# Pooled attention with a gated MLP on one core: the four hand-written issue lists are put in another order

## The chip, the core and the metric

The kernel runs on one core of a Trainium2 chip. The time is that of one execution on the device, in microseconds (us). The engines are PE (TensorE, matrix products; PEld is its weight load), DVE (VectorE), ACT (ScalarE), POOL (GpSimd) and SP (SyncE, which here issues nearly all DMAs). Each engine takes its own instructions strictly in the order in which the program lists them, and waits on semaphores for the results of the others.

## The reference

Eight batches of attention over pooled keys, then one gated MLP that mixes along the sequence. In the sizes of this case B = 8, H = 8, S = 576, D = 64, so x has 512 features:

```python
k_p = k.reshape(B, H, S // 8, 8, D).mean(axis=3)      # 72 keys a head
v_p = v.reshape(B, H, S // 8, 8, D).mean(axis=3)
scores = (q @ k_p.transpose(0, 1, 3, 2)) / sqrt(D)
attn = exp(scores - max(scores)); attn /= attn.sum(-1) + 1e-9
x = (attn @ v_p).transpose(0, 2, 1, 3).reshape(B, S, 512)
h = gelu_tanh(x @ w_in)                               # 512 x 1024
u, v = h[..., :512], h[..., 512:]
v_n = (v - mean(v)) / sqrt(var(v) + 1e-6) * g_ln
v_s = einsum('ts,bsd->btd', w_sg, v_n) + b_sg         # 576 x 576
out = x + (u * v_s) @ w_out                           # 512 x 512
```

Results are float32. The products that need it are made of high and low halves: an operand is split by ACT (the rounded high half) and by DVE or POOL (what is left), and three products are added in PSUM.

## The kernel before, in words

The work of one batch is cut into steps, and each step is a Python generator (`step_A` at line 359 to `step_Z` at line 900) that issues one stage up to each `yield`. The steps, with a number for the tile or head pair:

- A, B and C load a pair of k, of v, or a group of q; E loads the rows `left` over by the pooling (all DMAs go through `load`, line 211, on SP). lv, lu, lo, ls and lb load weights.
- K and P pool k and v: in batch 0 by PE, later by a DVE reduction (line 387). Q transposes q (on DVE at line 492, in batch 0 by PE at 484 with an ACT copy at 487).
- S makes the scores of two heads: five products into a PSUM tile, the negated maximum `nmax` on DVE (510), ten exponentials on ACT (529), then on DVE the sum, the reciprocal and the product `e` (538 to 547), after which the PSUM tile is given back; POOL copies the leftover columns `el` (555). Batches 0 and 1 use a variant with one large exponential.
- T transposes e on PE (161) and splits it with ACT `ah` (591) and DVE `al` (598); L does the same for the leftover columns. V multiplies with v; ACT copies the result out (626, 628), POOL takes the low half (630), ACT copies the end of the sequence to `xtails` (632).
- H is the product for one of five row tiles of the v half, 12 matmuls of 512 columns, followed by Gelu on ACT (669), the norm on DVE and POOL (674 to 680), and the split `vk` (ACT 683, POOL 685). U is the product of a quarter of the u half, 24 matmuls of 288 columns, followed by Gelu (700). Exp and Gelu need different activation tables, so a change from one to the other on ACT brings a table load.
- W is the product along the sequence, 28 matmuls of 288 columns, and the gating on DVE (744, 746; for the last batch 725 and 726, then a split by ACT 731 and POOL 734). G builds sums of the gated tiles for batches 1 to 6 on POOL and ACT (760 to 776), which let O make the output with seven products of half tiles instead of eight. O adds its products to x on DVE (832; batch 0 at 891, batch 7 at 868).
- Z transposes 128 columns of the output on DVE (910) and then issues four stores of 72 KB on SP. The buffer of the transpose is a quarter of `umem`, one for even and one for odd Z: Z3 can be transposed when the stores of Z1 have landed, Z2 when those of Z0 have.

The order is written out by hand in four lists at the top: PROLOGUE (batch 0 and the start of 1 and 2), FIRST (the rest of batch 1's period), PERIOD (issued for b = 2 to 6) and LAST (b = 7). A token names the step and, behind the sign, the batch relative to the list's own: `S3+1` is the next stage of step S3 of the next batch. Lower-case tokens prepare weights (`lv0` loads, `v0` is a stage of the split). A token whose batch lies outside 0 to 7, or whose step is finished, issues nothing. `emit` (939) walks a list and `advance` (919) or `weight` (925) issues the next stage, so that one list fixes the order on all engines at once. Dependencies that only order the issue then pin each engine to that order.

```python
free = [0, 1, 2, 3]
def take():
    n = free.pop(0)
    return n, psum.tile([P, 2, NB], F32, name="ps", tag=f"ps{n}")
def give(n):
    free.append(n)
```

There are four PSUM tiles of two banks. `take` (117) hands out the tile that was given back longest ago in the order of the list, and `give` (122) returns one. So the list also decides which step inherits whose tile: the first matmul of the new owner waits until the last reader of the former owner is done with it.

Of the kernel before, what the change touches and what calls it, by code (L numbers as in the profile page):

```python
# [20 lines left out]


PROLOGUE = """
lv0 E0+0 v0 A0+0 K2+0 A1+0 K0+0 C0+0 v0 v0 K1+0 v1 K0+0 v0 Q0+0 v1 C1+0 E1+0 v1 C3+0 K1+0 K2+0 P2+0 Q1+0 Q0+0 K2+0
S0+0 v0 S0+0 v1 Q1+0 S1+0 S0+0 Q3+0 S0+0 S1+0 C2+0 S1+0 S0+0 S0+0 Q2+0 Q3+0 ls0 S1+0 S0+0 S3+0 S0+0 S1+0 Q2+0 S2+0
S0+0 B1+0 S3+0 S3+0 S2+0 s4 v1 lv1 S3+0 S1+0 S1+0 s2 S1+0 T0+0 S2+0 s3 T0+0 s2 S2+0 S3+0 s3 S3+0 S3+0 S3+0 P1+0 s3 s2
s4 B0+0 A0+1 v3 S3+0 E0+1 S2+0 v3 s1 S1+0 v2 S2+0 S2+0 A1+1 S2+0 s1 s4 T3+0 C0+1 s1 P0+0 K0+1 S2+0 P2+0 T1+0 B0+1 K2+1
L0+0 T1+0 T2+0 v2 L0+0 V0+0 v3 V1+0 T2+0 K1+1 C1+1 V0+0 s0 V2+0 T3+0 v2 V1+0 s0 K2+1 v2 V0+0 v3 K2+1 V2+0 v2 Q0+1 lu0
V3+0 V0+0 V1+0 P0+1 s0 V1+0 S0+1 Q1+1 S0+1 S0+1 S1+1 C2+1 V3+0 S0+1 v3 S1+1 C3+1 V2+0 V3+0 u0 H0+0 u1 S1+1 u0 u1 S0+1
S1+1 H0+0 lu1 u1 u1 V2+0 S0+1 Q2+1 u0 S1+1 u0 S1+1 H2+0 V3+0 H2+0 u1 u0 H4+0 Q3+1 H1+0 S1+1 u3 H2+0 S0+1 H4+0 S3+1  # L30
T0+1 H4+0 S0+1 u2 u3 C0+2 H1+0 u2 lb0 H2+0 U1+0 H4+0 H3+0 u2 C1+2 T0+1 H4+0 u3 H1+0 u2 T0+1 u3 u3 B1+1 U1+0 P1+1 S3+1
P2+1 H3+0 S2+1 u2 H0+0 lo0 A0+2 S3+1 U3+0 S2+1 S3+1 S2+1 H3+0 S3+1 S2+1 S2+1 H0+0 U3+0 S3+1 H0+0 H4+0 U0+0 H3+0 S2+1
S1+1 H1+0 lo1 U2+0 S3+1 H2+0 H3+0 H4+0 H0+0 S2+1 H1+0 U0+0 U2+0 S3+1 S2+1 L0+1 L0+1 Q0+2 C2+2 K0+2 H1+0 L0+1 o1 T1+1
L0+1 H4+0 H2+0 H3+0 P2+1 o0 o1 o0 W3+0 P2+1 P2+1 W2+0 W3+0 o0 V0+1 W2+0 A1+2 o0 T1+1 o1 o1 o0 T1+1 o2 o1 W0+0 K1+2
V0+1 o2 T2+1 o2 o3 E0+2 V1+1 o2 W0+0 V1+1 o3 o3 W1+0 T2+1 K2+2 T2+1 V1+1 T3+1 Q1+2 K2+2 B0+2 W2+0 W0+0 K2+2 W3+0 W1+0
V2+1 T3+1 S0+2 W1+0 W2+0 S1+2 V2+1 W0+0 P0+2 W1+0 V1+1 Q2+2 S0+2 o3 O1+0 T3+1 S1+2 W3+0 O1+0 O1+0 B1+2 O0+0 S0+2 O0+0
o2 P1+2 S1+2 Z1+0 O0+0 O2+0 C0+3 V3+1 S0+2 S1+2 Z0+0 C3+2 V3+1 S2+2 A0+3 A1+3 O2+0 V0+1 P2+2 S0+2 V2+1 V3+1 H2+1 S2+2
o3 Q3+2 S2+2 V3+1 O2+0 Z0+0 H2+1 T0+2
""".split()
FIRST = """  # L40
A0+2 r0 K0+2 r0 P2+1 U2+0 r0 K1+2 H2+0 H1+0 S2+1 r0 B1+2 H3+0 H1+0 V0+0 S1-4 V2+0 Z2-1 P2+1 Z1-1 r0 H4+0 H1+0 H3+0
T0+1 H4+0 O3-1 r1 r1 r1 H3+0 Z1-11 U2+0 H1+0 H1+0 S2-3 O3-1 H2+0 A1-2 H4+0 H4+0 r1 O3-1 H1+0 H0+0 H4+0 Z3-1 Z2-1 S2+1
H3+0 H0+0 H0+0 Z3-1 U1+0 H4+0 S1+1 H3+0 S3+1 r3 S2+0 S3+1 H4+0 O0-3 P2+1 U1+0 H4+0 H3+0 U3+0 S3+1 W0-7 E0+2 H0+0 H0+0
S3+1 r3 Q3-5 H2+0 H0+0 H2+0 r3 U0+0 S0-2 Q0+2 r3 U3+0 W1+0 U0+0 T0-22 S3+1 W1+0 L0+1 C0-2 L0+1 r2 W0+0 W3+0 S1-5 r2 r2
K2+2 r2 r2 W0+0 L0+1 T0+1 W3-3 G1+0 V0+1 C1+2 W2+0 Q2-2 G0+0 P1+2 V0+1 T1+1 W3+0 L0+1 W2+0 G0+0 S0-1 G1+0 K2+2 O0+0
G1+0 T1+1 T1+1 K2+2 V0+1 W0-2 V1+1 P0-1 P2-7 T2+1 G2+0 O1+0 G4+0 V1+1 S0+2 W0-10 T2+1 O0+0 W1-5 G2+0 G2+0 G2+0 T2+1
V2+1 G2+0 V2+1 G3+0 Q1+2 G4+0 O1+0 O0+0 S2-3 G3+0 O1+0 S0+2 S0+2 G3+0 O0+0 O2+0 G4+0 C3+2 O1+0 T3+1 T3+1 V2+1 G4+0
O2+0 Z1+0 V3-1 G4+0 C2+2 T3+1 O0+0 W1-7 W2-7 O0+0 S1+2 V1+1 V3+1 Z0+0 Z1+0 S1+2 V3+1 O0+0 Z0+0 O0+0 V1-18 Z3+0 B0+2
Z2+0 W1+0 V3+1 Z3+0 Z2+0
""".split()  # L50
# [19 lines left out]


# [910 lines left out]
```

## Time and profile before

| | us |
|---|---|
| median of 3 runs (range) | 571.95 (571.55 to 572.54) |
| profiled execution, its own time | 572.45 |
| span of that execution | 570.4 |
| busy: PE, DVE, ACT, POOL | 544.5, 407.3, 371.5, 306.4 |

The span runs from the first to the last instruction of the profiled execution; some 2 us lie around it. A stretch that the text calls a period is one pass of PERIOD, measured from one batch's matmuls of 120 in a row to the next's. The granted clock of PE is 1.00 in every stretch with matmuls. In a timeline or a chain the columns are the start in us, the duration in us and the instruction, with a count where equal ones follow each other; square brackets give the idle time of the engine just before and what ended it.

### The profile page before, as it was taken

Reading aid. Unit: us, or ns where it says so; the run is one execution under the profiler, and the core shown is the slowest. Engines: PE = TensorE matmul, PEld = TensorE weight load, DVE = VectorE, ACT = ScalarE, POOL = GpSimd, SP = SyncE. Lnnn points to the kernel's source line nnn. Section 1 sums busy time; section 2 is a strip of 40 time slices with the busy share of each in tenths; the row PEclk is TensorE's granted clock in tenths of the full one; section 3 lists DMA queues with packets and bytes.
Section 4 is the critical chain, followed back from the end, with each engine's and each line's share of the span. In section 5 each row is a group of like instructions: output and inputs, shape, how many; then the busy total and the mean of one; then the engine's idle time right before and its main releaser. Section 6 shows DMA issues by size and latency. Waiting matters only on the chain.

```text
span 570.4 us, 10342 instructions
## 1 busy us (share of the span) xinstructions
PE 544.5 (95%) x3721; PEld 510.0 (89%) x3721; DVE 407.3 (71%) x591; ACT 371.5 (65%) x979; POOL 306.4 (54%) x366
## 2 busy tenths in 40 slices
...
GB/s 235 321 147 179 250 70 83 116 65 67 30 1 86 191 12 69 2 105 161 1 68 26 140 102 31 38 64 193 11 68 1 122 20 1 1 34 51 1 1 83
DMA packets 161602, 46.33 MB, mean 81 GB/s; under 512 B 149072, under 2 KB 149072, under 8 KB 161552
## 3 DMA queue, kind: packets, MB, share of 16 engines
...
q8 instruction: 29, 0.48, 0.4%
...
## 4 chain that ended last, share of the span: by engine, by line
PE 52%; DVE 18%; ACT 11%; DMA 6%; issue 5%; SPq 4%; POOL 3%; POOLq 0%; DVEq 0%; ACTq 0%
PE ps L126 49%; SPq L211 4%; DMA kvraw<-in_v 4%; ACT e L529 4%; DVE vp L387 2%; PE ps L161 2%; DVE nmax L510 2%; DVE e L547 2%; DVE ps L744 1%; ACT gk L760 1%; DVE qT L492 1%; DVE kp L387 1%; POOL umem L776 1%; ACT L529 1%; DVE al L598 1%
## 5 line engine op out<-in xcount | busy, mean ns | idle before, releaser
L126 PE MATMUL ps<-wsh,vk 128*128 128x288 f32 x512 | 97.1, 297 | 0.0
L126 PE MATMUL ps<-xhlk,wih 128*128 128x288 f32 x512 | 90.3, 299 | 3.0 <-DVE e L547 2.9
L126 PE MATMUL ps<-wih,xhlk 128*128 128x512 f32 x256 | 85.1, 399 | 1.3 <-DVE e L547 1.3
L126 PEld LDWEIGHTS ps<-xhlk,wih 128*128 128x128 f32 x512 | 75.3, 189 | 4.6 <-ACT vk L683 3.5
L529 ACT ACTIVATE e<-ps,nmax 128x72 f32<-128x72 f32 x240 | 72.9, 338 | 8.5 <-DVE nmax L510 8.3
L126 PEld LDWEIGHTS ps<-wsh,vk 128*128 128x128 f32 x512 | 78.2, 189 | 0.2 <-PE ps L126 0.2
L126 PEld LDWEIGHTS ps<-wih,xhlk 128*128 128x128 f32 x256 | 48.1, 188 | 13.5 <-DVE e L547 2.4
L126 PE MATMUL ps<-wsl,vk 128*128 128x288 f32 x256 | 57.4, 296 | 0.0
L126 PE MATMUL ps<-xhlk,wil 128*128 128x288 f32 x256 | 55.1, 297 | 0.0
L685 POOL TENSOR_TENSOR vk<-xmem,vk 128x512 fp32r<-128x512 f32 x32 | 41.3, 1297 | 25.6 <-ACT vk L683 25.6
L762 POOL TENSOR_TENSOR gk<-umem,gk 128x576 fp32r<-128x576 f32 x18 | 25.7, 1429 | 53.7 <-ACT gk L760 53.7
L529 ACT ACTIVATION_READ_ACCUMULATOR e<-ps,nmax 128x1 f32 x240 | 53.9, 225 | 0.0
L677 POOL TENSOR_TENSOR rstd<-mv,eps 128x1 f32<-128x1 f32 (+1 forms) x40 | 9.6, 241 | 79.2 <-DVE mv L675 75.9
L630 POOL TENSOR_TENSOR xhlk<-xmem,xhlk 128x576 fp32r<-128x576 f32 x32 | 45.4, 1427 | 11.4 <-ACT xhlk L628 11.4
L126 PE MATMUL ps<-wil,xhlk 128*128 128x512 f32 x128 | 50.7, 396 | 0.0
L126 PE MATMUL ps<-gk,woh 128*128 128x288 f32 x224 | 46.8, 300 | 0.6 <-POOL gk L734 0.3
L832 DVE TENSOR_TENSOR xmem<-ps,xmem 128x576 f32<-128x576 f32 x42 | 31.3, 756 | 20.6 <-PE ps L126 20.3
L126 PE MATMUL ps<-kbd,qT 128*128 128x144 f32 x320 | 43.9, 288 | 2.2 <-ACT qT L487 1.3
L126 PEld LDWEIGHTS ps<-kbd,qT 128*128 128x128 f32 x320 | 41.4, 190 | 3.9 <-ACT qT L487 1.7
L126 PEld LDWEIGHTS ps<-wsl,vk 128*128 128x128 f32 x256 | 42.2, 189 | 0.0
L126 PEld LDWEIGHTS ps<-xhlk,wil 128*128 128x128 f32 x256 | 41.1, 189 | 0.0
L762 POOL TENSOR_TENSOR vk<-umem,vk 128x576 fp32r<-128x576 f32 x24 | 34.0, 1426 | 8.0 <-ACT vk L760 7.0
...
## 6 DMA issues: line engine op xcount, KB each, us to landing
...
```

The costliest lines, as they stand in the source:

```text
L126: nc.tensor.matmul(o, lhsT, rhs, start=start, stop=stop, **flags)
L161: nc.tensor.transpose(ps[:rows, i * P:(i + 1) * P], src(i), ident if i < NT - 1 else swap)
L211: queue.dma_start(o, i)
L387: nc.vector.tensor_reduce(out=o, in_=t.rearrange("p a (r d) -> p a d r", r=POOL), axis=AX.X, op=ALU.add)
L510: nc.vector.tensor_reduce(out=nmax, in_=every.rearrange("p s (h k) -> p s h k", h=2), axis=AX.X, op=ALU.max, negate=True)
L529: nc.scalar.activation(e[:, i, h], slots[i][:, h], AF.Exp, bias=nmax[:, i, h:h + 1], **acc)
L547: (nc.gpsimd if (b, g) in MUL_POOL else nc.vector).tensor_tensor(e, e, rec.unsqueeze(3).broadcast_to([P, NT, 2, SP]), op=ALU.mult)
L630: nc.gpsimd.tensor_tensor(xhl[:, 1, g], x32[:, g], xhl[:, 0, g].bitcast(F32), op=ALU.subtract)
L677: nc.gpsimd.tensor_tensor(rstd, mv[:, 1:2], eps[:n, 1:2], op=ALU.add)
L685: (nc.gpsimd if i < NT - 1 else nc.vector).tensor_tensor(lo, vg, hi.bitcast(F32), op=ALU.subtract)
L762: nc.gpsimd.tensor_tensor(lo, x, hi.bitcast(F32), op=ALU.subtract)
L832: nc.vector.tensor_tensor(x, ps[:, :, 0:HALF], x, op=ALU.add)
```

## The change

The four lists are replaced by lists with another order of the same stages. No step, instruction, buffer or shape is changed; the tokens that issue nothing differ. PERIOD and LAST stand here in full, of PROLOGUE and FIRST the beginning.

```diff
--- before
+++ after
 PROLOGUE = """
-lv0 E0+0 v0 A0+0 K2+0 A1+0 K0+0 C0+0 v0 v0 K1+0 v1 K0+0 v0 Q0+0 v1 C1+0 E1+0 v1 C3+0 K1+0 K2+0 P2+0 Q1+0 Q0+0 K2+0
-S0+0 v0 S0+0 v1 Q1+0 S1+0 S0+0 Q3+0 S0+0 S1+0 C2+0 S1+0 S0+0 S0+0 Q2+0 Q3+0 ls0 S1+0 S0+0 S3+0 S0+0 S1+0 Q2+0 S2+0
-S0+0 B1+0 S3+0 S3+0 S2+0 s4 v1 lv1 S3+0 S1+0 S1+0 s2 S1+0 T0+0 S2+0 s3 T0+0 s2 S2+0 S3+0 s3 S3+0 S3+0 S3+0 P1+0 s3 s2
...
+lv0 v0 A1+0 E0+0 v1 A0+0 K1+0 C0+0 v0 K1+0 E1+0 v0 K0+0 K0+0 K2+0 K2+0 Q0+0 P2+0 K2+0 Q0+0 C1+0 v1 Q1+0 v0 S0+0 S0+0
+C2+0 v1 lv1 Q2+0 C3+0 Q1+0 v1 S1+0 S0+0 S1+0 v1 S0+0 Q2+0 S1+0 Q3+0 S0+0 S2+0 v0 S0+0 S0+0 S0+0 S1+0 S1+0 ls0 S2+0
+Q3+0 B1+0 S3+0 S1+0 v3 B0+0 T0+0 S2+0 S1+0 T0+0 s2 S0+0 s2 v3 v3 S1+0 E0+1 s1 S3+0 A0+1 S3+0 S2+0 s4 S3+0 s1 s4 P1+0
...
 """.split()
 FIRST = """
-A0+2 r0 K0+2 r0 P2+1 U2+0 r0 K1+2 H2+0 H1+0 S2+1 r0 B1+2 H3+0 H1+0 V0+0 S1-4 V2+0 Z2-1 P2+1 Z1-1 r0 H4+0 H1+0 H3+0
...
+H1+0 V0+0 Z2-1 H1+0 S1-1 S1+1 r0 Q3-6 P2-5 H3+0 C0-4 S3+1 r0 r0 H3+0 S2-1 K0+2 H1+0 V1-24 r0 V2+0 H2+0 O3-1 W0-13 S1-3
...
 """.split()
 PERIOD = """
-B1+1 Q2+1 H2+0 V2+0 S1+1 H2+0 S0+1 H1+0 S2+1 U3+0 H1+0 P0+1 S2+1 S0+1 Q3+1 C0+2 V3+0 S1+1 H1+0 V1+0 P1+1 H0+0 S2+1
-H2+0 T0+1 W1-13 U3+0 S1+1 H0+0 V0+0 T0+1 H1+0 S2+1 H2+0 S3+1 S3+1 H1+0 H4+0 S3+1 H0+0 H3+0 T0+1 H4+0 S3+1 U1+0 H4+0
-H1+0 H2+0 H2+0 S2+1 A0+2 H3+0 U0+0 P2+1 H3+0 H4+0 U2+0 U1+0 H4+0 P2+1 H0+0 K0+2 W0-9 H3+0 P2+1 H4+0 H0+0 U2+0 C1+2
-S3+1 L0+1 H3+0 H4+0 U0+0 L0+1 H0+0 H4+0 L0+1 P2+1 H3+0 W1+0 W1+0 W0+0 V0+1 Q0+2 W0+0 A1+2 W3+0 E0+2 K2+2 G0+0 K1+2
-W3+0 Q1+2 W2+0 G0+0 T1+1 G1+0 G1+0 V0+1 K2+2 T1+1 L0+1 W2+0 G2+0 G1+0 T1+1 K2+2 O0+0 V0+1 G2+0 T2+1 V1+1 G4+0 G2+0
-T2+1 O1+0 G4+0 T2+1 W2-10 V1+1 G2+0 G2+0 V2+1 T3+1 V2+1 O1+0 G3+0 O0+0 O1+0 O0+0 T3+1 T3+1 O0+0 O1+0 C2+2 O2+0 O0-4
-S0+2 O2+0 G3+0 Z1+0 S0+2 G4+0 G3+0 S1+2 B0+2 O0+0 Z0+0 O0+0 G4+0 Z1+0 V3+1 S0+2 V3+1 G4+0 Z0+0 W3-12 C3+2 V1+1 O0+0
-S1+2 O0+0 Z3+0 Z3+0 V2+1 V3+1 Z2+0 Z2+0
+S1+1 S0+1 S1+1 H2+0 H1+0 S1+1 Q2+1 S0+1 H2+0 H0+0 S1+1 S1+1 V2+0 V1+0 S2+1 V0+0 B0+1 V3+0 H0+0 H1+0 P1+1 S2+1 H1+0
+S2+1 P0+1 H3+0 H4+0 H1+0 H3+0 C0+2 U0+0 H2+0 H0+0 S2+1 C3+1 H2+0 U3+0 H4+0 T0+1 P2+1 U0+0 H4+0 A1+2 H4+0 P2+1 H2+0
+H4+0 P2+1 T0+1 S0+1 Q3+1 H3+0 U3+0 H0+0 H0+0 T0+1 H0+0 U1+0 H4+0 P2+1 H4+0 S3+1 H3+0 H1+0 H4+0 H1+0 U2+0 H3+0 C1+2
+K1+2 E0+2 U2+0 S3+1 S3+1 A0+2 U1+0 H2+0 H3+0 W1+0 S2+1 K0+2 S3+1 K2+2 S3+1 O0-1 W0-1 W0+0 L0+1 W0+0 W1+0 L0+1 G0+0
+L0+1 W2+0 K2+2 G1+0 W2+0 G0+0 K2+2 W3+0 G1+0 L0+1 T1+1 W3+0 G2+0 G1+0 V0+1 O1+0 T1+1 G2+0 W2-1 V0+1 G2+0 G4+0 G4+0
+T1+1 O1+0 G2+0 Q0+2 O0+0 T2+1 V1+1 O1+0 T2+1 T2+1 B1+2 T3+1 G2+0 V1+1 W1-9 O0+0 G3+0 G4+0 V2+1 T3+1 G3+0 W3-8 O0+0
+G4+0 T3+1 C2+2 O2+0 O0+0 G3+0 O0+0 O1+0 O2+0 V3+1 Z0+0 G4+0 S0+2 V1+1 O0+0 V2+1 Z0+0 V0+1 O0+0 Z1+0 V3+1 Q1+2 S0+2
+O0+0 Z1+0 Z3+0 Z2+0 V2+1 Z2+0 Z3+0 V3+1
 """.split()
 LAST = """
-S3+9 V1+0 T2+26 V3+0 H2+0 V0+0 H0+0 H0+0 V2+0 H1+0 V1-1 H1+0 C2-2 S3-1 L0+8 S3+1 B0+4 Q3-10 H4+0 H1+0 H1+0 H4+0 H1+0
-H0+0 P1+1 L0-1 H2+0 H1+0 H3+0 T1+12 S2-12 T2+7 S1+2 V2+5 S0+5 H2+0 T2+12 S2-11 Q2-8 H4+0 H0+0 U3+0 U3+0 H3+0 Q1+1 S0+6
-B1+12 U1+0 H3+0 H4+0 T1-20 V0-17 H0+0 V1+11 H4+0 S1+1 S0+1 U2+0 V1-4 V3+15 V3+10 V3-21 V2-3 T3-10 V0+3 H2+0 S2-15
-Q0+12 S1+5 C3+1 P2-10 K2+4 H3+0 H3+0 P2-2 H3+0 H4+0 U0+0 S3+11 H0+0 U2+0 T3-2 H4+0 K1+10 H2+0 L0+21 T3+14 H4+0 H2+0
-P2+1 A1-11 U0+0 L0+12 K2+24 U1+0 W0+0 W1+0 T0-12 W0+0 W2+0 S2-2 W2+0 W2+0 S0-12 W0+0 C1+4 W2+0 W0+0 W3+0 O1+0 S3-7
-W3+0 W1+0 O0+0 T0-14 S1+9 O1+0 W3+0 V2-10 W3+0 Z1+0 O0+0 W1+0 K0-5 V0+6 Z0+0 W1+0 K2+0 O0+0 Z0+0 A0+3 E0-13 C0+1 O3+0
-S0-11 O3+0 O1+0 S2+2 Z3+0 O2+0 P2-10 T0-12 T1+9 O3+0 S1+8 Z1+0 P0-1 Z3+0 O2+0 O2+0 Z2+0 Z2+0
+U2+0 H0+0 P1+9 V2+0 T2+6 V0-1 C0+8 Q2+4 P0+8 K2-1 H3+0 H3+0 L0+18 H3+0 H1+0 T3+7 V0+0 U2+0 H2+0 V3+0 L0+16 T1-24 K2+30
+V1+0 H1+0 S1+4 H1+0 S0+3 T1+7 H0+0 H0+0 H2+0 T0-20 H1+0 V3+9 H4+0 V0-17 T2+27 H2+0 H2+0 S2-18 H1+0 T0-20 B0+4 V1+15
+U1+0 S3+12 P2+4 H2+0 L0-4 H0+0 H3+0 H0+0 A1-8 H4+0 S1+2 T1+13 E0-15 H2+0 U1+0 H0+0 H3+0 K1+6 H4+0 U0+0 S3-10 K2+7 T3-5
+H3+0 V0+3 Q0-2 U3+0 H4+0 V1-5 C3-2 V3-13 H4+0 P2-23 H4+0 S0-23 U0+0 H4+0 H4+0 H1+0 S3-1 L0+13 W0+0 V3+17 T2+13 S3-19
+A0-2 S3+5 S0-7 S1+17 W1+0 W1+0 W0+0 U3+0 B1+25 W2+0 W0+0 W3+0 V2-9 S2-4 W0+0 W2+0 V2+5 S1+7 S2+0 S2-17 W2+0 V1-9 S1-1
+S2-6 W3+0 K0+9 Q3-5 W2+0 P2-5 W1+0 Q1+1 W3+0 O0+0 T0-14 O0+0 C1-1 O1+0 O1+0 Z1+0 T3+1 Z0+0 W1+0 W3+0 O3+0 V2+0 O0+0
+O1+0 Z1+0 C2-4 O3+0 S0+8 Z0+0 O3+0 O2+0 O2+0 Z3+0 Z3+0 O2+0 S0+16 Z2+0 P2-5 Z2+0
 """.split()
```

Three places that are hard to find in the lists: in PROLOGUE `A1+0` comes before `E0+0`, and `lv1` before `C3+0` and `ls0`; in PERIOD the end now runs `Z1+0` (transpose), `Q1+2`, `S0+2`, `O0+0`, `Z1+0` (stores), `Z3+0`, `Z2+0`; in LAST the four stages of `W0` (product, gate, and the split by ACT and by POOL) now come before the gate of `W2`, and the products are listed `O0 O0 O1 O1` where it was `O1 O0 O1 O0`.

## Rows read from the trace of the kernel before

**Rows 1.** Part 1 of the page: busy time of each engine and instructions.

```profile
PE 544.5 (95%) x3721; PEld 510.0 (89%) x3721; DVE 407.3 (71%) x591; ACT 371.5 (65%) x979; POOL 306.4 (54%) x366
```

**Rows 2.** Stretches: length, then busy PE, PEld, DVE, ACT, POOL, PEclk, DMA share, GB/s.

```profile
0.00:109.00 109.00, 93.50 (x634) 84.90 (x635) 93.91 (x125) 77.69 (x147) 72.14 (x100) 1.00 0.65 173
...
109.00:212.99 103.99, 102.67 (x695) 96.30 (x694) 75.13 (x113) 75.40 (x233) 64.79 (x77) 1.00 0.38 73
...
212.99:279.15 66.16, 65.04 (x451) 61.35 (x449) 48.64 (x70) 47.37 (x138) 32.49 (x38) 1.00 0.36 73
279.15:344.69 65.54, 65.31 (x451) 61.51 (x449) 49.18 (x71) 47.40 (x138) 32.85 (x39) 1.00 0.36 73
344.69:411.75 67.06, 65.72 (x451) 61.41 (x449) 49.18 (x71) 47.50 (x138) 32.84 (x39) 1.00 0.36 72
411.75:478.08 66.33, 65.32 (x451) 61.52 (x449) 48.29 (x72) 47.49 (x138) 33.15 (x39) 1.00 0.25 46
250.00:260.00 10.00, 10.00 (x60) 8.92 (x59) 8.25 (x14) 9.48 (x41) 1.28 (x5) 1.00 0.82 143
...
478.08:566.00 87.92, 86.96 (x606) 82.99 (x603) 42.13 (x74) 28.66 (x53) 38.10 (x39) 1.00 0.16 24
```

**Rows 3.** Waits of PE, whole span: us in total, times, longest.

```profile
PE ps L126 <- DMA kvraw<-in_k: 8.4, 1, 8.4
PE ps L126 <- DVE e L547: 4.2, 5, 1.1
PE ps L126 <- ACT qT L487: 1.3, 2, 1.0
```

**Rows 4.** Chain of waits at 345 us, and the commonest matmul on the page.

```profile
344.94 16.09 PE ps L126 x120
...
L126 PE MATMUL ps<-wsh,vk 128*128 128x288 f32 x512 | 97.1, 297 | 0.0
```

**Rows 5.** SP's timeline to 4.2 us, and the chain of waits there: start, us.

```profile
1.24 1.60 SPq L211 DMA_DIRECT2D left<-in_k  x2
2.89 1.91 SPq L211 DMA_DIRECT2D kvraw<-in_k  x3
...
3.55 4.74 DMA kvraw<-in_k
...
8.43 5.26 PE ps L126 x32
```

**Rows 6.** Chain of waits from 396 to 405.6 us.

```profile
397.95 0.82 DVE nmax L510
...
398.85 1.28 ACT L529
...
400.14 3.14 ACT e L529 x20
...
403.77 0.92 DVE e L547
```

**Rows 7.** PE's timeline at 404 us; in brackets its idle time and the releaser.

```profile
404.82 0.76 PE L126 MATMUL ps<-xhlk,wih 128*128 128x288 f32 x4 [1.00 <-DVE e L547]
```

**Rows 8.** Stores and transposes: timelines of SP and DVE, chain of waits.

```profile
243.57 4.25 SPq L211 DMA_DIRECT2D out<-umem  x8
...
249.51 1.44 DVE L910 STREAM_TRANSPOSE umem<-xmem 128x576 f32<-128x576 f32 x2
...
379.37 3.87 DMA out<-umem
...
383.42 0.78 DVE L910 STREAM_TRANSPOSE umem<-xmem 128x576 f32<-128x576 f32 x1 [1.06 <-DMA out<-umem]
```

**Rows 9.** PE's timeline at 506 and at 552 us.

```profile
506.72 1.46 PE L126 MATMUL ps<-vk,wbk 128*128 128x288 f32 x9 [0.37 <-POOL vk L762]
...
552.36 0.53 PE L126 MATMUL ps<-gk,woh 128*128 128x288 f32 x2 [0.32 <-POOL gk L734]
```

**Rows 10.** Part 2 of the page: GB/s moved, in 40 slices of the span.

```profile
GB/s 235 321 147 179 250 70 83 116 65 67 30 1 86 191 12 69 2 105 161 1 68 26 140 102 31 38 64 193 11 68 1 122 20 1 1 34 51 1 1 83
```

More of the change, by code (lines that the diff above doesn't have):

```diff
@@ L23 @@
 PROLOGUE = """
-lv0 E0+0 v0 A0+0 K2+0 A1+0 K0+0 C0+0 v0 v0 K1+0 v1 K0+0 v0 Q0+0 v1 C1+0 E1+0 v1 C3+0 K1+0 K2+0 P2+0 Q1+0 Q0+0 K2+0
-S0+0 v0 S0+0 v1 Q1+0 S1+0 S0+0 Q3+0 S0+0 S1+0 C2+0 S1+0 S0+0 S0+0 Q2+0 Q3+0 ls0 S1+0 S0+0 S3+0 S0+0 S1+0 Q2+0 S2+0
-S0+0 B1+0 S3+0 S3+0 S2+0 s4 v1 lv1 S3+0 S1+0 S1+0 s2 S1+0 T0+0 S2+0 s3 T0+0 s2 S2+0 S3+0 s3 S3+0 S3+0 S3+0 P1+0 s3 s2
-s4 B0+0 A0+1 v3 S3+0 E0+1 S2+0 v3 s1 S1+0 v2 S2+0 S2+0 A1+1 S2+0 s1 s4 T3+0 C0+1 s1 P0+0 K0+1 S2+0 P2+0 T1+0 B0+1 K2+1
-L0+0 T1+0 T2+0 v2 L0+0 V0+0 v3 V1+0 T2+0 K1+1 C1+1 V0+0 s0 V2+0 T3+0 v2 V1+0 s0 K2+1 v2 V0+0 v3 K2+1 V2+0 v2 Q0+1 lu0
@@ L29 @@
[L29 to L38, printed above, removed]
+lv0 v0 A1+0 E0+0 v1 A0+0 K1+0 C0+0 v0 K1+0 E1+0 v0 K0+0 K0+0 K2+0 K2+0 Q0+0 P2+0 K2+0 Q0+0 C1+0 v1 Q1+0 v0 S0+0 S0+0
@@ new lines @@
+C2+0 v1 lv1 Q2+0 C3+0 Q1+0 v1 S1+0 S0+0 S1+0 v1 S0+0 Q2+0 S1+0 Q3+0 S0+0 S2+0 v0 S0+0 S0+0 S0+0 S1+0 S1+0 ls0 S2+0
+Q3+0 B1+0 S3+0 S1+0 v3 B0+0 T0+0 S2+0 S1+0 T0+0 s2 S0+0 s2 v3 v3 S1+0 E0+1 s1 S3+0 A0+1 S3+0 S2+0 s4 S3+0 s1 s4 P1+0
+v2 P0+0 s2 P2+0 S2+0 S2+0 S3+0 S2+0 s3 S3+0 s0 S3+0 S2+0 s3 v3 S3+0 S1+0 s4 S2+0 s1 C1+1 T2+0 K2+1 A1+1 S3+0 s3 s0
+T1+0 T1+0 lu0 L0+0 s0 v3 L0+0 Q1+1 T3+0 V1+0 T3+0 v2 K0+1 K1+1 V0+0 C0+1 V1+0 T2+0 V3+0 u1 u1 v2 K2+1 Q0+1 v2 B0+1
+K2+1 V1+0 V0+0 lu1 v2 u1 V0+0 V2+0 S0+1 V2+0 V3+0 P0+1 S1+1 S0+1 V2+0 B1+1 S1+1 S0+1 V3+0 u0 H1+0 H0+0 S0+1 S1+1 u1
```

25 lines of the change are left out of this document (17 added, 8 removed).

## The prediction

> **What bounds the kernel now.** The first part of the page [rows 1] has PE busy for 95% of the span. No other engine comes near, so the reader should ask not which engine is slow but where PE has no work: 570.4 − 544.5 = 25.9 us. The table of stretches [rows 2] places them: 15.5 us up to 109 us, 1.3 up to 213, 1.1, 0.2, 1.3 and 1.0 in four successive periods, 1.0 from 478 to 566; what is left, 4.4, lies behind the last product. The waits of PE [rows 3] name causes. The first 8.4 us is a k tile that has not landed. Next come 4.2 us on `DVE e L547`, the end of a softmax, which gives a PSUM tile back; eleven smaller rows follow, the largest 1.3 us. In the first 109 us DVE is as full as PE (93.9 of 109), so there the order on DVE also counts.
>
> The busy figure hides part of a wait. 120 matmuls of 288 columns take 16.09 us [rows 4], 134 ns apart, but the record of one lasts 297 ns, so the modelled end covers some 0.16 us of every gap. With about three short waits per period the true loss is 0.93 + 3 × 0.16 = 1.4 us per period (0.93 is the mean of the four). That is what an order can win.
>
> **The change, part by part.** No instruction is added or removed, and walking the Exp and Gelu activations of both orders gives 38 table loads each. So the floor of PE stays, and only its waits can change.
>
> *Start.* SP issues, before the first k tile, the 1 MB weight (lv0) and two `left` transfers in 1.60 us; the tile lands 4.74 us after its last issue and PE begins at 8.43 [rows 5]. The new list issues A1 right behind lv0 and only then E0 and A0, and PE pools A1's tile first. Its issue comes 1.6 us earlier; its data still stand behind the 1 MB, and its own pair of 0.5 MB takes as long as before. I take −1.0. Bounds: 0 (the megabyte decides alone) and −1.6.
>
> *Rest of PROLOGUE.* Up to the first product of attention with v, the old list puts 26.2 us of work on DVE and the new one 24.5 (my count from the order and the durations in the trace). Between there and the W tiles the new order is by turns ahead and behind, and at the first W the two are within 0.5 us. So DVE leads early only; I take −1.5, the early lead. Bounds: −4, a bit over half of the 7.1 us that PE idles between 8.43 and 109 [rows 2]; and +3.3, priced in rival B. In FIRST one product of batch 0 (O3) inherits a PSUM tile from an H tile with short cover: +0.5, between 0 and +1.
>
> *The period, five times.* `take` hands out the tile that was given back longest ago, so the list decides who waits for whom. Old: U0 inherits the tile of S3. Between S3's matmuls and U0 PE has 8.8 us of other work (its cover; covers are the matmuls that the list puts between, at the pitch of [rows 4] and of their like). Against it stand nmax 0.82, a table load of 1.28, the exponentials 3.14, the division and product that end with 0.92, with other DVE work in between [rows 6]. U0 stands 1.00 us for it [rows 7]. New: S3's tile goes to W2 with 11.2 us of cover, S1's to H3 with 9.1, S2's to T0 with 12.0; that wait and a 0.26 us wait of V for `al` go. What comes instead:
> S0's tile goes to H0 with only 7.9 us of cover, and the chain is long. Z1's stores are issued right ahead of Z3's transpose, which reuses their buffer. On DVE behind Z3's transpose come Z2's, S1's nmax, Q2, and only then S0's product. From the end of S0's matmuls: SP is free of Z0's stores at about 0.4, issues Z1's four in 2.1 (eight take 4.25 [rows 8]), the last beginning at 2.0; when that has landed come two transposes of 0.78, the maximum 0.82, a transpose of much the same length, and 1.2 us (the 0.92 and two small ones, estimated). With a landing of 2.1 us the product ends at 8.4: H0 waits 0.5. How long a store takes to land the trace only bounds. In one period two transposes ran together at 249.51, no wait ahead of either, where the last of eight issues began at about 247.3: at most 2.9. In another the landing took 3.87 and DVE stood 1.06 for it [rows 8]. I take 2.1, under the first bound since that transpose did not wait at all; 0 and 3.87 stay for the range (no wait, or 2.3 us).
> The Trainium skill's page DMA: Bandwidth & Descriptors, section Anatomy of one DMA, calls some 2.0 us of setup and completion approximately constant; by it alone H0 would wait about 0.4 us in each period and the sum would be half a microsecond lower. The row of 3.87 speaks against a constant.
> Next, S2 inherits H2's tile: H2's gelu stands on ACT behind two rows of exponentials and two table loads, 0.25 us late. O1 waits some 0.3 us for G1's POOL difference. Together 1.05 against 1.4: −0.35, five times −1.75. Bounds per period: −1.4 and +1.45 (the long landing).
>
> *The end of batch 6 and LAST.* The wait at 506.72 [rows 9] disappears, as the POOL step for that product stands further ahead: −0.5. In LAST W0 is gated and split before W2 is gated, and the products run O0 O0 O1 O1: the wait at 552.36 [rows 9] and two too short for the list go, with the hidden part about −0.95. Bounds: 0 and −1.3. The 4.4 us behind the last product stay: gather, transpose, store are the same.
>
> **Sum.** −1.0 − 1.5 + 0.5 − 1.75 − 0.5 − 0.95 = −5.2. The profiled execution took 572.45 (span 570.4 and 2.05 around it), so 567.25; it is 0.5 over the median of 571.95, so against the median 566.75, given as 566.7.
>
> **Rivals.**
> A, slower: the stores land late in every period, not in one of four. The place is Z3's transpose, the price 1.8 us a period, 9 in all: about 575.7. It takes the five periods' gain once the landing exceeds 2.45 us and the whole gain at about 3.1. For: the 3.87; and SP issues more loads around it. Against: three of the four periods show no wait, though at most 2.9 us were there.
> B: a worse prologue. The new list issues lv1, 1 MB, ahead of a q group and the spatial weights; at the 321 GB/s of the second slice [rows 10] these come up to 3.3 us later. If S3 of batch 0 or the casts stand for it, about 570. For: DVE is nearly full there and can't catch up. Against: S0 to S2 supply work meanwhile.
> C: nothing measurable, the waits change their owner (the same 1.4 us per period under other names) and the prologue, bound by PE and DVE together, gives nothing: about 571.5.
> D: a deeper gain. The prologue wins its 4 us and the periods lose nearly nothing: about 560.5. It needs all covers to hold.
> E: the load row, not the matmul row, is the floor. By it, 510.0 of PEld [rows 1], 12.8 for the start and the end, and 2.05 around the span would allow 525. The stretch from 250 to 260 us shows PE 10.00 and PEld 8.92 [rows 2]: full without a pause, with 11% of PEld idle; so no order gets there. The Trainium skill's Perfetto Trace Analysis, section Identifying the Most-Contended Engine, judges headroom by that load share; the trace of this stretch does not bear it out.
>
> **How the numbers follow.** Forecast (563 to 568.8) 0.48; B (568.8 to 570.8) 0.16; D (below 563) 0.12, of which 0.05 below 560.5; C 0.10; A 0.08, other mishaps of the reshuffled prologue with a loss 0.05; E 0.01. What a measurement of this kernel can tell from no change is about 0.2%, 1.1 us. Faster: 0.48 + 0.16 + 0.12 + 0.01 = 0.77; same 0.10; slower 0.13. The range runs from 560.5 to 572.5: D to its value and C are in, the slower cases, E and the rest of D, 0.19, out.
>
> **What would show it.** Right: first matmul near 7.4 us; the wait on `DVE e L547` under 2 us in all; periods of 65.7 to 66.1; no wait at O in batch 6's end. Wrong: `DMA out<-umem` before L910 in most periods with H waiting for L547 (A); PE idle over 15 us up to 109 (B); the same sum of waits under new names (C). The forecast falls if the periods stay at 66.3 or the prologue gains nothing.

## The result

The changed kernel takes 564.54 us (median of 4 runs, 563.87 to 564.87) where the kernel before took 572.25 (4 runs, 571.55 to 573.53): a ratio of 0.9861, 95% interval 0.9841 to 0.9882, 7.7 us less. The forecast was 5.2 us less; the result lies in the range, and between the forecast and rival D.

The profiled execution of the changed kernel took 564.37 us with a span of 562.6. First its page: the span, part 1 (compare [rows 1]), and of part 5 the group of L126 that waited longest.

```profile
span 562.6 us, 10338 instructions
...
PE 541.5 (96%) x3721; PEld 510.2 (91%) x3721; DVE 416.3 (74%) x591; ACT 373.0 (66%) x979; POOL 309.2 (55%) x366
...
L126 PE MATMUL ps<-wih,xhlk 128*128 128x512 f32 x256 | 84.9, 401 | 2.5 <-DVE e L547 2.4
```

Two things are to be read here. PE's idle time fell from 25.9 to 562.6 − 541.5 = 21.1 us, 4.8 of the 7.8 by which the span fell. The other 3.0 is a fall of PE's busy time, though it ran the same 3721 instructions: PE loses time under a record that still runs. By the distances between matmuls (the table below) about half of it is the hidden part of waits, which the prediction had added by hand, and the other half gaps so short that no idle time shows; the first 32 matmuls, which took 0.79 us longer, count against it. And L547 now delays only 512-column matmuls (steps H); before, three of its five waits delayed the 288-column ones of U.

The stretches of the changed kernel, in the columns of [rows 2]; the last four are the second to the fifth pass of PERIOD, from one end of W to the next:

```profile
0.00:109.00 109.00, 96.44 (x650) 87.95 (x651) 94.15 (x128) 79.58 (x164) 69.96 (x100) 1.00 0.70 178
109.00:208.00 99.00, 98.89 (x668) 92.79 (x667) 74.80 (x107) 68.10 (x196) 66.03 (x73) 1.00 0.36 68
...
225.84:292.25 66.41, 64.92 (x450) 61.30 (x450) 51.03 (x71) 47.89 (x137) 33.60 (x38) 1.00 0.36 72
292.25:357.17 64.92, 64.47 (x451) 61.32 (x450) 51.05 (x71) 47.88 (x137) 33.71 (x38) 1.00 0.36 74
357.17:423.80 66.63, 64.91 (x451) 61.28 (x450) 50.97 (x71) 47.88 (x137) 33.60 (x38) 1.00 0.36 72
423.80:487.80 64.00, 64.00 (x447) 61.06 (x447) 45.24 (x68) 46.95 (x133) 33.60 (x38) 1.00 0.22 37
```

The first 109 us idle 12.6 us instead of 15.5, the next stretch hardly at all. But the periods are of two kinds: 65.2 us or less, and 66.4 to 66.6. Measured alike, the five passes take 65.2, 66.4, 64.9, 66.6 and 64.0 us, where before they took 64.7, 66.3, 65.5, 67.1 and 66.2: the long ones are hardly shorter than before, and most of the gain is in the fifth. What makes the long ones is in the waits of PE, with the columns of [rows 3]:

```profile
PE ps L126 <- DMA kvraw<-in_k: 7.5, 1, 7.5
PE ps L126 <- DVE e L547: 2.4, 2, 1.2
PE ps L126 <- ACT qT L487: 1.6, 3, 0.7
PE ps L126 <- DVE e L520: 1.0, 1, 1.0
PE ps L161 <- ACT umem L700: 1.0, 3, 0.5
```

`DVE e L547` is down from five waits to two, and each is longer. DVE's timeline where Z3 and Z2 are transposed (L910), in two periods:

```profile
247.34 1.44 DVE L910 STREAM_TRANSPOSE umem<-xmem 128x576 f32<-128x576 f32 x2 [2.94 <-DMA out<-umem]
...
312.11 1.44 DVE L910 STREAM_TRANSPOSE umem<-xmem 128x576 f32<-128x576 f32 x2 [1.30 <-DMA out<-umem]
```

And the last leg of Z1's stores there, in the chain of waits:

```profile
243.53 3.59 DMA out<-umem
...
309.94 2.05 DMA out<-umem
```

Where the last store lands in 2.05 us, DVE stands 1.30 us and H0 does not wait. Where it lands in 3.59, DVE stands 2.94 and PE stops 1.23 us in H0 at 251.66. In the third of the four stretches SP needed 2.02 us for one issue and DVE stood 2.89, and PE stopped 1.17 us. The chain of the prediction is there, and rival A came true in two of the five periods.

The late landing is not a matter of chance. The trace has the start of every DMA packet, and 29 of 16 KB each stand on a queue of their own, which the page lists among the DMA queues (packets, MB, share of 16 engines):

```profile
q8 instruction: 29, 0.48, 0.4%
```

One of them starts at 244.1 us, within the late landing, and one at 374.3, with the slow issue; none starts among the stores of the other three periods. The late landing of the kernel before (379.37, [rows 8]) has one at 380.1. Five of the runs below keep the place of Z3 and Z2 in PERIOD. In them and in the changed kernel DVE stands 2.5 to 3.2 us in the same two passes, each time with such a packet in the 4.5 us before, and 0.7 to 1.4 us in the other three, each time without. That the packet holds the stores up is read from this coincidence; no run moves it by itself.

To see what each list gave, one number per stage was worked out from the traces: take the start of each matmul, the distance to the next one, and subtract what is usual for its kind (the same line, tiles and shape; the shortest of the medians in the twelve traces). What is left is the time that PE lost, the start included.

| PE's lost time, us | up to the end of W, batch 1 | from there to the end of W, batch 6 | behind it | sum |
|---|---|---|---|---|
| before | 25.6 | 12.0 | 2.3 | 40.0 |
| changed | 22.2 | 9.4 | 0.5 | 32.1 |
| new PROLOGUE alone | 23.7 | 11.6 | 2.3 | 37.6 |
| new FIRST and PERIOD alone | 25.9 | 10.0 | 1.7 | 37.5 |
| new LAST alone | 25.0 | 11.4 | 1.1 | 37.5 |

So the change gains 3.4, 2.6 and 1.8 us in the three stages. By pass of PERIOD, PE lost 1.1, 2.7, 2.0, 3.5 and 2.7 us before and 1.4, 2.9, 1.4, 3.1 and 0.7 in the changed kernel: 2.0 of the 2.6 us come from the fifth pass. There nothing of a batch 8 is loaded or pooled (DVE is busy 45.2 us instead of 51.0), and neither H0 nor L0 waits. The first stage varies from 21.4 to 23.0 us in six traces with the changed kernel's PROLOGUE and order of FIRST up to there, so tenths mean nothing in it.

### The profile page after: what moved, and what is told of

It is laid out like the page before. It is cut to its first block, busy times and chain, and to the rows that moved or that the text cites. A ratio compares the mean times of both kernels' runs of the same rounds, so it can differ in the third digit from the quotient of the medians.

```text
span 562.6 us, 10338 instructions
## 1 busy us (share of the span) xinstructions
PE 541.5 (96%) x3721; PEld 510.2 (91%) x3721; DVE 416.3 (74%) x591; ACT 373.0 (66%) x979; POOL 309.2 (55%) x366
## 4 chain that ended last, share of the span: by engine, by line
PE 58%; DVE 17%; ACT 6%; DMA 5%; issue 5%; SPq 4%; POOL 4%; DVEq 0%; ACTq 0%; POOLq 0%
PE ps L126 54%; SPq L211 4%; PE ps L161 3%; DMA kvraw<-in_v 2%; ACT e L529 2%; DVE xmem L680 2%; DVE bst L674 2%; DVE kp L387 2%; DVE nmax L510 2%; DMA out<-umem 1%; DVE vk L685 1%; DVE qT L492 1%; POOL xhlk L630 1%; POOL gk L754 1%; DVE e L547 1%
## 5 line engine op out<-in xcount | busy, mean ns | idle before, releaser
L126 PE MATMUL ps<-wsh,vk 128*128 128x288 f32 x512 | 97.6, 298 | 0.0
L126 PE MATMUL ps<-xhlk,wih 128*128 128x288 f32 x512 | 90.2, 298 | 0.5 <-ACT xmem L669 0.5
L126 PE MATMUL ps<-wih,xhlk 128*128 128x512 f32 x256 | 84.9, 401 | 2.5 <-DVE e L547 2.4
L126 PEld LDWEIGHTS ps<-wsh,vk 128*128 128x128 f32 x512 | 78.0, 188 | 0.1
L126 PEld LDWEIGHTS ps<-xhlk,wih 128*128 128x128 f32 x512 | 75.4, 188 | 1.6 <-ACT xmem L669 0.9
L126 PEld LDWEIGHTS ps<-wih,xhlk 128*128 128x128 f32 x256 | 48.0, 188 | 14.4 <-issue 3.2
L126 PE MATMUL ps<-wsl,vk 128*128 128x288 f32 x256 | 57.4, 295 | 0.0
L126 PE MATMUL ps<-xhlk,wil 128*128 128x288 f32 x256 | 55.1, 297 | 0.0
L555 POOL COPY el<-e 128x40 f32<-128x40 f32 x64 | 13.4, 262 | 74.0 <-DVE e L547 73.6
L685 POOL TENSOR_TENSOR vk<-xmem,vk 128x512 fp32r<-128x512 f32 x32 | 46.8, 1487 | 7.7 <-ACT vk L683 7.7
L126 PE MATMUL ps<-wil,xhlk 128*128 128x512 f32 x128 | 50.5, 395 | 0.0
L776 POOL TENSOR_TENSOR umem<-umem 128x576 f32<-128x576 f32 x24 | 34.1, 1429 | 23.2 <-DVE umem L746 22.6
L126 PE MATMUL ps<-kbd,qT 128*128 128x144 f32 x320 | 45.0, 288 | 1.6 <-ACT qT L487 1.6
L126 PE MATMUL ps<-gk,woh 128*128 128x288 f32 x224 | 46.1, 296 | 0.0
L126 PEld LDWEIGHTS ps<-kbd,qT 128*128 128x128 f32 x320 | 41.7, 190 | 4.1 <-ACT qT L487 2.1
L126 PEld LDWEIGHTS ps<-wsl,vk 128*128 128x128 f32 x256 | 42.1, 188 | 0.0
L126 PEld LDWEIGHTS ps<-xhlk,wil 128*128 128x128 f32 x256 | 41.0, 188 | 0.1
L598 DVE TENSOR_TENSOR al<-ps,ah 128x576 fp32r<-128x576 f32 x28 | 21.2, 756 | 26.3 <-ACT ah L591 26.0
```

Source lines behind the costliest of these rows:

```text
L126: nc.tensor.matmul(o, lhsT, rhs, start=start, stop=stop, **flags)
L555: nc.gpsimd.tensor_copy(st["el", b].rearrange("p t (n j a) -> p t n j a", n=2, a=4)[:, :, g // 2, :, 2 * (g % 2) + h], ef[:, :, LEFT[h]:LE ...
L598: nc.vector.tensor_tensor(al, ps[:, 0:S], ah.bitcast(F32), op=ALU.subtract)
L685: (nc.gpsimd if i < NT - 1 else nc.vector).tensor_tensor(lo, vg, hi.bitcast(F32), op=ALU.subtract)
L776: nc.gpsimd.tensor_tensor(x, p, q, op=ALU.subtract)
```

## The experiments

Diffs of the first three are against the kernel before, the others against the changed kernel. Where an edit moves Z2, Z3 or B0, the ends of FIRST and LAST were changed alike; of PERIOD the lines with the edit are shown. Ratios are to the kernel before, timed on the same chip: 572.40 us, and 572.49 in the runs with nmax alone and with the old start. The changed kernel was timed beside a kernel before of 572.25 us; differences from it are of bare medians and carry this shift of 0.15 to 0.24 us.

**One list at a time.** Every list ends with the same stages done in both versions, apart from FIRST, which goes with PERIOD. So they can be exchanged singly.

```diff
-PROLOGUE of the kernel before
+PROLOGUE of the changed kernel
```

> Only PROLOGUE is new. Theory (each list takes its own waits of PE away, and the gains add up): the first matmul at 7.5 us instead of 8.4, PE some 2.1 us ahead where PROLOGUE ends, and nothing gives it back: 2.1 us less than the kernel before, about 570. Rival (a lead is absorbed, since the next tile or DVE, which is as full as PE there, holds PE up anyway): 0 to 0.5 us less, about 572. Rival B of the prediction (the megabyte ahead of the q group costs time): 1 us more.

Measured: 568.55 us, ratio 0.9930 (0.9909 to 0.9951), 3.9 us less, more than either theory; the profiled execution lost 2.4 us less than before. Its first matmul comes at 7.4 us. The gain is not absorbed, but it is not won where the theory had it: up to the end of W in batch 0 the profiled execution lost 22.8 us, as before. The old FIRST loses less (between the ends of W in batches 0 and 1 PE loses 0.9 us instead of 2.8, and the waits of 1.1 us on L547 and 0.4 on L598 there are gone). Part of what the old FIRST stood for was work of PROLOGUE. The timed runs fall in two pairs, 567.56 and 567.60, 569.50 and 569.87, and the profiled execution is the last of these; the median therefore gains 1.5 us more than it. What parts the pairs is left open.

```diff
-FIRST and PERIOD of the kernel before
+FIRST and PERIOD of the changed kernel
```

> Only FIRST and PERIOD are new. Theory: the rest of batch 1 and the five periods give what the traces show between these points, 1.2 and 2.6 us: about 568.3. In two or so of the five periods H0 still waits over 1 us for the product of S0 (stores landing late); L547 before U0 is gone. Rival (the periods gain only because they start in another phase behind the new PROLOGUE): 0 to 1 us less.

Measured: 569.10 us, ratio 0.9937 (0.9922 to 0.9952), 3.3 us less. The periods gain by themselves, 2.0 us in the table, and two waits on L547 are there as in the full change. The rival falls.

```diff
-LAST of the kernel before
+LAST of the changed kernel
```

> Only LAST is new. Theory: the waits at 506 and 552 us go, 1.5 to 1.85 us less, about 570.3. Rival (the wait at 506 us belongs to the end of the last PERIOD and not to LAST): 0.9 us less, with the wait on L762 still there.

Measured: 570.17 us, ratio 0.9968 (0.9951 to 0.9984), 2.2 us less (0.9 to 2.8 by the interval, which covers both theories); behind the last W of batch 6 the table shows 1.2. Of the two waits of [rows 9] one is left, as the rival had it; the waits of PE:

```profile
PE ps L126 <- DVE e L547: 3.9, 5, 1.1
...
PE ps L126 <- POOL vk L762: 0.4, 1, 0.4
```

The wait on L762 belongs to the end of the last PERIOD (it is gone where PERIOD is new), the one on L734 to LAST. The three gains add up to 9.4 us in medians and to 7.4 in lost time, against 7.7 and 7.9 for all together: they add, within the noise of three medians. One overlap shows: between the ends of W in batches 0 and 1 the new PROLOGUE alone takes 1.9 us, the new FIRST alone 1.0, and both together 2.1.

**Z3 and Z2 later.** If H0 waits because Z3's transpose stands for Z1's stores in front of S0's product on DVE, the two transposes can go behind that product.

```diff
 PERIOD
-S1+1 S0+1 S1+1 H2+0 H1+0 S1+1 Q2+1 S0+1 H2+0 H0+0
+S1+1 S0+1 S1+1 H2+0 H1+0 S1+1 Q2+1 S0+1 Z3-1 Z2-1 Z2-1 Z3-1 H2+0 H0+0
...
-O0+0 Z1+0 Z3+0 Z2+0 V2+1 Z2+0 Z3+0 V3+1
+O0+0 Z1+0 V2+1 V3+1
```

> The new lists, but the transposes Z3 and Z2 and their stores stand behind the product of S0 of the next batch. Theory (H0's wait of 1.3 us in two of five periods is Z3's wait for the stores of Z1, passed on by DVE to the product of S0): DVE waits on out<-umem fall from 12.5 us to under 3, PE's wait on L547 from 2.4 us to under 0.5, and the time by 2.5 us against the changed kernel, about 562. Rival (the product of S0 comes late because of the exponentials on ACT): the wait on L547 stays over 1.5 us and the time within 0.5 us of the changed kernel, 564.5.

Measured: 577.32 us, ratio 1.0080 (1.0060 to 1.0099), 12.8 us slower than the changed kernel. Yet of the theory's own signs one appeared, no wait on L547, and the other nearly: DVE's wait for stores is down to 3.7 us in one place (under 3 was expected), and that place is behind the periods. Something else took their place. The waits of PE:

```profile
PE ps L161 <- ACT umem L700: 7.1, 4, 2.3
PE ps L161 <- POOL el L555: 2.3, 1, 2.3
```

And the wait of DVE for a v tile, span and all (11.0 us of it in the periods):

```profile
DVE vp L387 <- DMA kvraw<-in_v: 15.0, 6, 3.2
```

PE's timeline at the first of these waits of PE:

```profile
219.97 0.60 PE L161 MATMUL ps<-ident,el 128*64 128x128 f32 x4 [2.27 <-ACT umem L700]
```

And the stretch behind it, in the columns of [rows 2]:

```profile
220.68:226.00 5.32, 5.32 (x31) 5.32 (x31) 4.39 (x7) 3.19 (x5) 1.10 (x1) 0.68 0.00 2
```

Moving Z2 and Z3 moved their eight stores too, and these now stand on SP later, still ahead of B0, the load of the next v tile. B0 begins 9.1 us after the batch's first H matmul (at 258.34 and 249.27 us) where in the changed kernel, in a period without a late store, it is 6.9 (317.83 and 310.98). DVE reaches the reduction of that tile and waits 2.3 us with everything behind it: nmax of S3, then on ACT the exponentials, a table load and the Gelu whose PSUM tile L0 inherits. And the wait costs more than it lasts: the 28 matmuls of W behind it took 5.25 us where the next 28 took 3.73, at a granted clock of 0.68 in that stretch, between the two levels of 1.2 and 2.4 GHz.

**B0 ahead of the stores.** First alone, then with the late transposes.

```diff
 PERIOD
-V0+0 B0+1 V3+0
+V0+0 V3+0
...
-O0+0 Z1+0 Z3+0 Z2+0 V2+1 Z2+0 Z3+0 V3+1
+O0+0 Z1+0 B0+2 Z3+0 Z2+0 V2+1 Z2+0 Z3+0 V3+1
```

> The new lists, with the load of the first v pair (B0) issued right behind the stores of Z1, 16 stages earlier. Theory (in the changed kernel DVE waits only 0.2 us for this tile, so its place on SP's queue does not matter there): within 0.5 us of the changed kernel, 564.5, and H0 still waits over 1 us in two of the five periods or so. Rival (the load's place bounds the periods already in the changed kernel): 1.5 us less or more.

Measured: 563.88 us, ratio 0.9852 (0.9834 to 0.9870), 0.7 us under the changed kernel and hardly outside the half microsecond allowed, with intervals that overlap; H0 still waits 1.9 us in two places. The load's place is next to free there.

```diff
 PERIOD
-S1+1 S0+1 S1+1 H2+0 H1+0 S1+1 Q2+1 S0+1 H2+0 H0+0 S1+1 S1+1 V2+0 V1+0 S2+1 V0+0 B0+1 V3+0
+S1+1 S0+1 S1+1 H2+0 H1+0 S1+1 Q2+1 S0+1 Z3-1 Z2-1 Z2-1 Z3-1 H2+0 H0+0 S1+1 S1+1 V2+0 V1+0 S2+1 V0+0 V3+0
...
-O0+0 Z1+0 Z3+0 Z2+0 V2+1 Z2+0 Z3+0 V3+1
+O0+0 Z1+0 B0+2 V2+1 V3+1
```

> B0 as in the run before, and Z3 and Z2 behind the product of S0 as in the run that was 12.8 us slower. Theory (that run lost its time because the eight stores of Z2 and Z3 then stood later on SP's queue, ahead of B0, and DVE waited 11 us for the tile, which delayed S3 and through ACT the Gelu that gives a PSUM tile to L0): DVE's wait for the v tile in the periods is gone, PE's wait of L161 on L700 falls from 7.1 to 1 to 3 us, its wait on L547 is under 0.5, and the time is 562, 2.5 us under the changed kernel. Rival (the two transposes in their new place on DVE are what delays S3): the time stays over 570.

Measured: 560.71 us, ratio 0.9796 (0.9776 to 0.9815): 3.8 us under the changed kernel and 16.6 under the run with late transposes alone, by moving one load. L547 has left the list; L161 on L700 remains, 1.1 us in four waits. That settles both: H0's wait was the stores', and the 12.8 us were B0's place on SP.

**nmax ahead of a reduction.** From B0's tile on DVE is busy without a pause up to nmax of S3 (in the changed kernel from 257.9 to 275.6 us), and the 2 us of K1 stand just before it. First on top of the lists of the run before:

```diff
 PERIOD
-C1+2 K1+2 E0+2 U2+0 S3+1 S3+1 A0+2
+C1+2 E0+2 U2+0 S3+1 S3+1 K1+2 A0+2
```

> As the run before, and nmax and the exponentials of S3 ahead of the reduction of K1 on DVE. Theory (what is left of the wait of L161 on L700, 0.4 to 0.7 us in each period of the changed kernel, is 2 us of K1 in front of nmax on a DVE that is full from B0's tile on): that wait under 0.5 us in all, and 1.5 to 2.5 us less than the run before, about 560. Rival (the exponentials wait for U2's Gelu on ACT anyway): no difference.

Measured: 559.37 us, ratio 0.9768 (0.9743 to 0.9794), 1.3 us under the run before it, a little less than expected; by the distances between matmuls the periods gain 1.9. The wait on L700 is gone from the list. The periods are now full; two of them as stretches:

```profile
290.46:354.69 64.23, 64.23 (x450) 61.48 (x450) 51.16 (x71) 47.89 (x137) 33.59 (x38) 1.00 0.37 75
354.69:418.94 64.25, 64.25 (x450) 61.49 (x450) 51.22 (x71) 47.88 (x137) 33.56 (x38) 1.00 0.37 75
```

PE is busy for the whole of each. By the distances between matmuls it still loses 0.7 us in each, so another order of these instructions can take little more out of a period. The same move alone, in the changed kernel:

> The new lists, only the reduction of K1 behind nmax and the exponentials of S3. Theory (PE's wait of L161 on L700 is K1 ahead of nmax on DVE, and it is a loss of its own beside H0's wait): that wait under 0.3 us in all, 1.5 to 2.5 us less than the changed kernel's 564.5, L547 still 2 to 2.5 us. Rival (in the periods where H0 waits, the other wait is only moved, since DVE then has the slack): 0 to 0.7 us less.

Measured: 561.75 us, ratio 0.9814 (0.9799 to 0.9829), 2.8 us less; by the distances between matmuls the periods gain 2.4. The wait of L161 on L700 is gone from the list, and so is the one of 0.4 us on L555; L547 is still 2.1 us in two places, and DVE still stands 12.3 us for stores. So it is a loss of its own, and bigger than the 1.4 us that the list of waits shows, since part of each wait is hidden. The prediction had not seen it.

**The megabyte, and the start.**

```diff
 PROLOGUE
-C2+0 v1 lv1 Q2+0 C3+0
+C2+0 v1 Q2+0 C3+0
...
-Q3+0 B1+0 S3+0
+Q3+0 B1+0 lv1 S3+0
```

> The new lists, with the megabyte lv1 behind ls0 and B1, as it stood before. Theory (the q group and the spatial weights came early enough): within 1 us of the changed kernel, 564.5. Rival B of the prediction (the megabyte costs PE time): PE idle up to 109 us falls by 1 us or more from the 12.6 of the changed kernel, and the time with it, about 563.

Measured: 565.58 us, ratio 0.9881 (0.9859 to 0.9903), 1.0 us more than the changed kernel; PE idles 13.0 us up to 109. So moving the megabyte up had cost nothing that shows, and rival B falls. Nor need the microsecond be the load's: of four runs two took 564.6 and 564.9 us at a granted clock of 1.000 over the whole run, and two 566.3 and 566.4 at 0.997 and 0.995. The profile is of the longest, and shows where the clock was lower. PE's timeline where it pools v, and the stretch there:

```profile
29.07 5.46 PE L126 MATMUL ps<-early,apart 128*128 128x128 f32 x32 [1.15 <-DVE e L520]
```

```profile
29.07:34.60 5.53, 5.53 (x35) 5.53 (x36) 5.40 (x8) 3.75 (x7) 5.19 (x8) 0.69 0.80 194
```

The same in the changed kernel:

```profile
28.19 3.84 PE L126 MATMUL ps<-early,apart 128*128 128x128 f32 x32 [1.05 <-DVE e L520]
```

```profile
28.19:32.10 3.91, 3.91 (x35) 3.91 (x36) 3.81 (x7) 3.77 (x7) 3.56 (x5) 1.00 0.92 209
```

In both PE had waited for L520, 1.15 and 1.05 us. In the one the granted clock was then 0.69, between its two levels, and the 32 matmuls took 5.46 us; in the other 1.00 and 3.84. Whether the load's place has a part in that is not shown; the changed kernel's own four runs have 0.999 to 1.000.

```diff
 PROLOGUE
-lv0 v0 A1+0 E0+0 v1 A0+0 K1+0 C0+0 v0 K1+0 E1+0 v0 K0+0 K0+0
+lv0 v0 E0+0 A0+0 v1 A1+0 K0+0 C0+0 v0 K0+0 E1+0 v0 K1+0 K1+0
```

> The new lists, but SP begins as before: lv0, E0, then the first k pair, which PE pools first. Theory (the lead of 0.9 us at the first matmul is given back at once, since the first 32 matmuls take 6.05 us in the changed kernel and 5.26 before): first matmul near 8.4 us, the 32 end within 0.3 us of the 13.6 us of the changed kernel, and the time within 0.5 us of its 564.5. Rival (the prediction's first term: each of the 0.9 us counts): about 565.4.

Measured: 565.13 us, ratio 0.9877 (0.9861 to 0.9894), 0.6 us more than the changed kernel, between the two theories. Against the kernel before beside each it is 7.4 us less where the changed kernel was 7.7, and the two intervals overlap, so the times do not decide between them. PE's timeline at the first matmuls ([rows 5] has those of before):

```profile
8.32 5.61 PE L126 MATMUL ps<-kvraw,apart 128*128 128x128 f32 x32 [8.32 <-DMA kvraw<-in_k]
```

And in the changed kernel:

```profile
7.51 6.05 PE L126 MATMUL ps<-kvraw,apart 128*128 128x128 f32 x32 [7.51 <-DMA kvraw<-in_k]
```

The first 32 matmuls end at 13.93 and 13.56: of a lead of 0.81 us 0.37 is left. Against the kernel before it is 0.13 of 0.92. But the earlier start is not what takes the lead back. The run with nmax alone has the same PROLOGUE:

```profile
7.36 5.16 PE L126 MATMUL ps<-kvraw,apart 128*128 128x128 f32 x32 [7.36 <-DMA kvraw<-in_k]
```

It starts 0.15 us earlier than the changed kernel and is through 1.04 us earlier. The 32 matmuls begin 213 ns apart up to a point and 111 ns apart from there on, and the point differs: 12.2 us in the changed kernel, 11.5 before, 10.2 in this run. 213 ns is the pace at the lower of the two levels of the clock, as the run with the late megabyte shows; a stretch at the start of the changed kernel, and one of that run at a granted clock of 0.50, both with 128-column matmuls:

```profile
8.00:11.00 3.00, 3.00 (x16) 3.00 (x15) 1.91 (x1) 0.00 (x0) 0.93 (x1) 1.00 1.26 239
...
30.00:33.00 3.00, 3.00 (x16) 3.00 (x16) 2.90 (x6) 2.78 (x5) 2.73 (x4) 0.50 0.79 208
```

The 1.00 of the first is no reading: the trace's entries on the clock begin at the point of the change (12.20 us here), and what comes before counts as full. So the clock is not 1.00 in every stretch with matmuls, as was said ahead of the prediction. In the eight traces with the new PROLOGUE's start, the 32 begin at 7.4 to 8.2 us and end at 12.5 to 14.3; in the four with the old start they begin at 8.3 to 8.4 and end at 13.7 to 14.5. The ends scatter by about as much as the lead or more, so two profiled executions can't tell what the earlier start is worth.

## Why the prediction was right, and where it was not

The sign, the place (PE's waits and nothing else) and the manner (PSUM tiles with longer cover) were right: the matmuls are the same, U0's wait for S3's tile is gone from the three periods that had it, and each list gains by itself. The sum came out nearer than its terms, some of which were off in opposite directions. By the steps:

- *Start, −1.0.* The first matmul came 0.92 us earlier, as forecast. But the step took the first matmul for the end of the stage: behind it PE runs for 2.8 to 5.6 us at the lower level of the clock, and in the two executions compared 0.13 us of the lead remains behind the first 32 matmuls. What the lead is worth is not shown; undoing it costs 0.6 us or less, within the noise.
- *Rest of PROLOGUE −1.5, FIRST +0.5.* With the start −2.0 were forecast and −3.4 came, the largest miss. Two terms were off, in opposite directions. Up to the end of W in batch 0 PE lost 22.2 to 24.1 us in three traces with the old PROLOGUE and 20.7 to 22.8 in seven with the new: by the means 1.4 less, where start and rest together had 2.5. From there to the end of W in batch 1 it lost 2.8 us before and 0.7 in the changed kernel: 2.1 less, where 0.5 more was forecast. The part that failed is the sentence that DVE's early lead is all: the new PROLOGUE alone takes 1.9 us from the waits in the old FIRST. The +0.5 for O3's short cover did not show; PE idles 0.11 us in the stretch from 109 to 208.
- *Rival B.* The megabyte cost nothing.
- *The period, −1.75.* −2.6 were measured, but not as −0.35 five times: +0.3, +0.2, −0.6, −0.4 and −2.0. Of the five passes none lies in the 65.7 to 66.1 us named as a sign, two lie over the 66.3 at which the forecast was to fall, and the waits on L547 are 2.4 us in all, not under 2. That the total is near is in part luck: the last pass made up for the others. H0's wait with its chain (Z1's stores, Z3, Z2, nmax, Q2, product) was right, and it vanishes with Z3 moved; a late landing costs 1.2 us, less than the 2.3 forecast for 3.87. With a landing of 2.05 us, though, H0 waits for nothing: the 0.5 us forecast for it was the chain's length, taken a little too long. A wait of L0 for a Gelu was missed, 0.4 to 0.7 us in four of the periods by the distances between matmuls.
- *Hidden parts of waits.* The reading that each wait costs more than its idle time held: 3.0 us of the gain appear as less busy time. The 1.4 us per period that an order could win was too small, though: in the same four periods PE lost 2.7 us on average by the distances between matmuls, and 0.65 in the version with full periods.
- *End of batch 6 and LAST, −1.45.* 1.8 were measured, 1.2 of it LAST's own and the wait at 506 PERIOD's.
- *Rival A* was the right mechanism with too small a share of periods to turn the sign. The share is fixed: the same two passes are late in all six traces with Z3 in this place.
- *Rival E.* In the version with full periods PE is busy 64.23 of 64.23 us while PEld is at 61.48: what is full is the matmul row, with 0.7 us still lost in it by the distances between matmuls.

The Trainium skill's page DMA: Bandwidth & Descriptors, section Anatomy of one DMA, gives some 2.0 us of fixed time for DMAs that GpSimd issues. The stores here are issued on SP. The 2.05 us at 309.94 lie near that figure all the same, and the 3.59 us at 243.53 show that it is not all one has to allow for.
